# Segment-recurrent attention with streamed weights: a ring of six places and 21 units, and four output units inside the last values pass

## The chip, the cores and the metric

The kernel runs on one core of a Trainium2 chip. The metric is the device time of one execution in microseconds (us), the median of several runs. A core has a matrix engine (TensorE, PE in the profile, with its weight loads as PEld), a vector engine (DVE), a scalar engine (ACT), GpSimd (POOL) and SP, which only issues DMAs here. Results of TensorE land in PSUM banks and are moved to the on-chip memory (SBUF) by DVE or ACT; this is called evicting below.

## The reference

For x of 2048 tokens by 1024, xn is its layer norm, and the result is x + A(xn) + B(xn). B is a feed-forward block with gelu (1024 to 3584 and back). A is attention with a memory that is carried along:

```
for s in range(n_seg):                     # 64 segments of 32 tokens
    h = concat([mem, xs])                  # 8 memory rows + 32 tokens = 40 rows
    q, k, v = h Wq, h Wk, h Wv             # 32 heads of 128
    p = softmax(mask(q k^T / sqrt(128)))
    o = (p v) Wo                           # 4096 to 1024
    mem = o[:8]                            # memory of the next segment
    outs.append(o[8:])
```

The next segment needs mem, so the 64 segments run one after the other, and each reads all of Wq, Wk, Wv and Wo (32 MB in bf16).

## The kernel before

A first stage computes the layer norm and B and lays the normalised rows out for the segments (hr_d in device memory). Then come the 64 segments, which the change touches.

**Units.** The four weight matrices are cut into 64 units of 128 x 2048 (512 KB): K, Q and V have 8 units (i) in each of two halves of the heads (u), O has 16. ORDER (L46) is the order of use in a segment: K, Q, V of half 0, K, Q, V of half 1, then all of O. 44 units stay in SBUF; 20, marked S in PLACED, are streamed from device memory in every segment through a ring of STREAM_BUFS = 5 places. Ring places and resident units share the same SBUF, so one place more is one resident unit less. When a streamed unit has been used, unit_done calls start_stream (L185): SP issues the DMA of the unit five further on in the list into the place just left (L193). One streamed unit, IN_PSUM, the fourth of the list, is not fetched by DMA but copied out of PSUM by ACT (L190) and then DVE (L191).

**Rows.** Each pass works on 32 rows: the 8 memory rows and 24 of the segment's tokens. The other 8 tokens of each segment ("left" rows) don't feed the memory, and are worked on for four segments at once. With i4 the segment's number modulo 4, the left rows add a second product per unit to K (i4 = 0), to Q (2), to V (3), and make the O products twice as wide (1).

**A segment.** half_pass (L588) multiplies the rows hT by the 8 units of one matrix and half: four matmuls of 512 columns per unit side by side on TensorE (L598). `at` is a list of calls made after a given unit. Passes are evicted by rows_out (ACT, L626) or left_out (DVE, L632). turn_k and turn_q transpose (L555, L642, L652); scores multiplies q and k and takes the exponential on ACT (L696); sums adds them up, takes logarithm and exponential on ACT (L708, L709) and scales on DVE (L710, L711); values multiplies by v (L722, L728) and evicts with ACT and DVE (L734, L735). o_product (L746) adds the 16 O units up in one accumulator, psX. At the end L841 (ACT) and L842 (DVE) evict psX, L222 transposes, and L223 writes the new memory rows into hT; the next segment's K pass starts there. L847 adds the residual.

**Accumulators.** Four PSUM banks are handed out by new_acc and taken back by let_go, first in, first out. A pass whose bank has just been left waits until its eviction has ended.

**Around the change.** Each engine runs its instructions in the order in which the code writes them. Before, turn_q comes after V3 of the half 1 (the unit with i = 3), scores(1) after V6; then V is evicted on DVE, the next segment's rows are loaded on POOL's queue (load_x_rows, L201), and the O units follow, with sums after O1, values(1, 0) after O5, values(1, 1) after O7. load_res (L808) loads the residual, on POOL's queue with i4 of 0 and 3, on ACT's (after O8) with 1 and 2.

Of the kernel before, what the change touches and what calls it, by code (L numbers as in the profile page):

```python
# [17 lines left out]
S = 2048  # L18
# [23 lines left out]


NUNIT = 64
STREAMED = 20
STREAM_BUFS = 5  # L46


def pass_order():

    order = []

    for u in range(2):
        for w in ("K", "Q", "V"):
            for i in range(KT):
                order.append((w, i, u))
    for ch in range(2):
        for j in range(4):
            for u in range(2):
                order.append(("O", ch * 4 + j, u))  # L60
    return order


ORDER = pass_order()
PLACED = "S...S..." "S...S..S" "...S..S." "..S...S." ".S..S..S" "..S..S.." "S..S..S." ".S..S..S"
IS_STREAMED = {unit: PLACED[n] == "S" for n, unit in enumerate(ORDER)}
assert PLACED.count("S") == STREAMED
RESIDENT = [unit for unit in ORDER if not IS_STREAMED[unit]]
# [6 lines left out]
def kernel(  # L75
# [16 lines left out]
    nc = tc.nc  # L92
# [106 lines left out]
    def load_x_rows(s, eng=nc.sync):  # L199
        hr = hrp.tile([P, 256], BF16, name="hr")  # L200
        eng.dma_start(out=hr[:, :], in_=hr_d[s, :, 0:256])  # L201
        nxt["hT"] = hr.rearrange("p (k t) -> p k t", k=KT)
# [290 lines left out]
    with tc.tile_pool(name="late", bufs=1) as late, \  # L493
# [10 lines left out]
        def new_acc():  # L504
            bank = free_banks.popleft()
            ps = banks.tile([P, 512], F32, name="acc", tag=bank)
            bank_of[id(ps)] = bank, ps
            return ps
# [48 lines left out]
        def by_head(t):  # L557
            return t.rearrange("p c (j t) -> p (c j) t", j=4)

        O_UNITS = ORDER[48:]  # L560

        hT, hL = nxt["hT"], nxt["hL"]
        kL, VL = [None] * 2, [None] * 2
# [3 lines left out]
        for s in range(NSEG):  # L567
# [18 lines left out]
            st = {}  # L586

            def half_pass(w, u, left, at, lead=0):  # L588


                ps = new_acc()
                psL = new_acc() if left else None
                ahead = [i for i in range(KT) if not IS_STREAMED[w, i, u]][:lead] if left else []
                order = ahead + [i for i in range(KT) if i not in ahead]

                def product(i, t, lhs, acc, seq):
                    for j in range(4):
                        nc.tensor.matmul(  # L598
                            acc[32 * j:32 * j + 32, :],
                            lhsT=lhs[:, i, :],  # L600
                            rhs=t[:, 512 * j:512 * j + 512],
                            start=(i == seq[0]),
                            stop=(i == seq[-1]),
                            tile_position=(0, 32 * j),
                        )

                for i in ahead:
                    product(i, unit_tile((w, i, u)), hL, psL, order)
                for i in range(KT):
                    t = unit_tile((w, i, u))  # L610
                    product(i, t, hT, ps, range(KT))
                    if left and i not in ahead:
                        product(i, t, hL, psL, order)
                    if first and (w, i, u) == IN_PSUM:
                        keep_unit(t)
                    unit_done((w, i, u))
                    for fn in at.get(i, ()):
                        fn()
                return ps, psL
# [10 lines left out]
            def left_out(psL, tag, pool=sp):  # L630
                nat = home(tag, pool)
                nc.vector.tensor_copy(out=nat[:, :], in_=psL[:, :])  # L632
                let_go(psL)
                return nat

            def left_values(u, ps):
                VL[u] = left_out(ps, f"VL{u}", late)
# [11 lines left out]
            def turn_q(nat):  # L649
                turn4(nat, tr)  # L650
                st["qT"] = HOME["b"].rearrange("p (h q) -> p h q", q=40)
                nc.vector.tensor_copy(out=st["qT"][:, :, 0:32], in_=by_head(tr))  # L652

            def turn_qL(nat, u):
                turn4(nat, qL[:, 4 * u:4 * u + 4, :])

            def q_left(u):

                if i4 == 3 and more:
                    q = qS[:, u, :, :]  # L660
                else:
                    q = by_head(qL[:, 4 * u:4 * u + 4, :])[:, :, NL * i4:NL * i4 + NL]
                nc.vector.tensor_copy(out=st["qT"][:, :, 32:40], in_=q)

            def keep_q(u):

                nc.vector.tensor_copy(
                    out=qS[:, u, :, :], in_=by_head(qL[:, 4 * u:4 * u + 4, :])[:, :, 3 * NL:4 * NL]
                )

            def scores(u):

                kT, qT = st["kT"], st["qT"]
                sA = mixed[:, 0:160].rearrange("p (c q) -> p c q", q=40)
                sB = mixed[:, 160:224].rearrange("p (c q) -> p c q", q=16)
                for n, (o, m) in enumerate((
                    (sA[:, :, 0:NX], mask_order[:, None, 0:NX].to_broadcast([P, 4, NX])),
                    (sB, mask_seg[:, i4:i4 + 1, None].to_broadcast([P, 4, 16])),
                    (sB[:, :, 8:16], mask_order[:, None, NL * i4:NL * i4 + NL].to_broadcast([P, 4, NL])),
                )):  # L680
                    nc.tensor.matmul(o, lhsT=ident[:, :], rhs=m, start=(n == 0), stop=False, skip_group_check=True)
                for c in range(4):
                    for j in range(4):
                        q = slice(32 * j, 32 * j + 32)
                        nc.tensor.matmul(
                            sA[q, c, :], lhsT=kT[:, 4 * c + j, :], rhs=qT[:, 4 * c + j, :],
                            start=False, stop=True, skip_group_check=True, tile_position=(0, 32 * j),
                        )
                    for j in range(4):
                        q = slice(32 * j, 32 * j + 32)  # L690
                        nc.tensor.matmul(  # L691
                            sB[q, c, :], lhsT=kL[u][:, 4 * c + j, :], rhs=qT[:, 4 * c + j, NX:40],
                            start=False, stop=True, skip_group_check=True, tile_position=(0, 32 * j),
                        )
                pr = sp.tile([P, 224], BF16, name="pr", tag="e")
                nc.scalar.activation(out=pr[:, :], in_=mixed[:, 0:224], func=ACT.Exp, scale=INV_SQRT_DH)  # L696
                st["pr"] = pr
# [92 lines left out]
                at[6].append(lambda: left_values(0, psVL))  # L790
            psQ1, psQ1L = half_pass("Q", 1, left_q, at)
            natq1 = rows_out(psQ1, "b")
            at = {3: [lambda: turn_q(natq1)], 6: [lambda: scores(1)]}
            if first:
                at[3].append(lambda: st.update(natL=left_out(psQ1L, "VL1", late)))
                at[5] = [lambda: turn_qL(st["natL"], 1), lambda: q_left(1)]
            else:
                at[3].append(lambda: q_left(1))
            if left_o:
                def load_resL():  # L800
                    st["resL"] = sp.tile([P, 256], BF16, name="resL", tag="qS")
                    nc.gpsimd.dma_start(out=st["resL"][:, :], in_=hrL_d[og, :, 256:512])

                at[3].append(load_resL)

            def load_res(tag, eng):
                st["res"] = sp.tile([P, 256], BF16, name="res", tag=tag)
                eng.dma_start(out=st["res"][:, :], in_=hr_d[s + 1, :, 256:512])  # L808
# [1 line left out]


            if i4 in (0, 3) and not final and not first:
                at[4] = [lambda: load_res("qS", nc.gpsimd)]
            psV1, psV1L = half_pass("V", 1, left_v, at)
            st["V"] = left_out(psV1, "a")
            if first:
                left_values(1, psV1L)
            if not final:
                load_x_rows(s + 1, nc.gpsimd)


            at = {1: [sums], 5: [lambda: values(1, 0)], 7: [lambda: values(1, 1)]}
            if left_v and not first:
                at[7].append(lambda: left_values(1, psV1L))
            if left_q and not first:
                at[8] = [lambda: keep_q(1), lambda: st.update(natL=left_out(psQ1L, "d"))]
                at[11] = [lambda: turn_qL(st["natL"], 1)]
            psX = new_acc()
            for n, unit in enumerate(O_UNITS):
                t = unit_tile(unit)  # L830
                o_product(unit, t, psX)
                unit_done(unit)
                for fn in at.get(n, ()):
                    fn()
                if n == 8 and not st.get("res"):
                    load_res("e", nc.scalar)
            nw = 2 if left_o else 1
            if not final:
                o_sb = HOME["d"]
# [83 lines left out]
```

## Time and profile before

| what | value |
|---|---|
| median of 3 runs | 2337.02 us (2333.44 to 2340.34) |
| profiled execution, its own time | 2337.02 us |
| its span, first to last instruction | 2335.2 us |
| TensorE busy | 2072.1 us (89%) |
| DVE, ACT, POOL busy | 841.4, 656.1, 269.5 us |
| streamed and resident fetches on SP's queue | 703.15 MB of 728.35 MB |
| mean DMA rate over the span | 312 GB/s |

A group line of the profile names line, engine, operation, output and inputs, then count, busy time and mean length, then the idle time before it and what ended it. A wait line reads: who waited <- for whom: total us, times, longest. A line of the timeline is start, length, engine, line, operation, and in brackets the idle time before it and its releaser. The chain of work that ended last is followed back from the last instruction; "DMA u<-Wc_Q" is a streamed Q unit on its way into the ring (u).

### The profile page before, as it was taken

The page shows a single profiled execution, that of the slowest core. Times are in us where ns is not written, and L with a number is a line of the kernel's source. Part 1 is how long each engine was busy: PE and PEld are TensorE (multiplying, and loading weights), DVE is VectorE, ACT ScalarE, POOL GpSimd, SP SyncE. Part 2 cuts the span into 40 slices and gives each one's busy share as a digit, 9 for nine tenths or more (in the row PEclk, how much of TensorE's full clock was granted, in tenths as well). Part 3 has the DMA queues.
Part 4 walks back from the last instruction along what each step waited for, and adds up shares of the span by engine and source line. Part 5 has one row for each costly group of instructions (what it writes and reads, how often), then busy time and mean ns, then how long its engine had stood idle before and what let it go on. Part 6 is the DMA issues. An engine that isn't in the chain of part 4 may idle for free.

```text
span 2335.2 us, 78748 instructions
## 1 busy us (share of the span) xinstructions
PE 2072.1 (89%) x34687; PEld 1063.2 (46%) x34707; DVE 841.4 (36%) x2311; ACT 656.1 (28%) x1540; POOL 269.5 (12%) x527
## 2 busy tenths in 40 slices
PE   7999999888888889898889888888888888898986
PEld 3444444344444444444444444444444444444443
DVE  6574753233333333333323233333333333333332
ACT  5261532122222222222222222222222222222222
POOL 0000000033101010111010101010101111111111
PEclk9999999999999999999999999999999999999999
DMA  9521117899999999999999999999999999999997
GB/s 324 181 69 44 43 51 263 305 374 376 348 345 358 349 344 365 353 360 357 347 343 361 324 340 354 355 355 357 350 341 346 350 352 343 353 350 359 371 345 273
DMA packets 247412, 728.35 MB, mean 312 GB/s; under 512 B 49899, under 2 KB 67259, under 8 KB 247068
## 3 DMA queue, kind: packets, MB, share of 16 engines
q1 hardware_dynamic: 225532, 703.15, 82.5%
q0 software_dynamic: 16000, 16.87, 2.2%
q8 instruction: 271, 4.44, 0.7%
q10 hardware_dynamic: 5536, 3.30, 0.5%
q14 instruction: 73, 0.60, 0.1%
HBM read 708.96 MB, written 32.57 MB: 318 GB/s over the span
## 4 chain that ended last, share of the span: by engine, by line
PE 57%; DMA 33%; ACT 4%; DVE 4%; issue 2%; POOL 0%; ACTq 0%; POOLq 0%; SPq 0%; DVEq 0%
PE acc L598 26%; DMA u<-Wc_Q 13%; DMA u<-Wc_O 10%; PE ps L391 8%; PE ps L438 6%; DMA u<-Wc_K 6%; PE acc L746 6%; DMA u<-Wc_V 4%; PE mixed L555 3%; PE acc L722 2%; PE ps L471 2%; ACT u L190 1%; ACT d_oL L735 1%; ACT d_oL L734 1%; DVE u L191 1%
## 5 line engine op out<-in xcount | busy, mean ns | idle before, releaser
L598 PE MATMUL acc<-u,hr 128*32 128x512 bf16 x12288 | 968.5, 400 | 91.3 <-DMA u<-Wc_Q 36.4
L598 PEld LDWEIGHTS <-hr 128*32 128x32 bf16 x12288 | 327.5, 99 | 422.2 <-issue 179.0
L598 PE MATMUL acc<-u,hrL 128*32 128x512 bf16 x3072 | 305.6, 389 | 2.0 <-ACT xtok L484 1.1
L626 ACT CAST d_oL<-acc 128x512 bf16<-128x512 f32 x192 | 112.5, 586 | 477.6 <-PE acc L598 416.2
L391 PE MATMUL ps<-u 128*128 128x512 bf16 x896 | 196.5, 382 | 2.6 <-ACT u L297 2.6
L642 DVE COPY kT<-mixed 128x512 bf16<-128x512 bf16 x128 | 54.4, 425 | 362.8 <-PE mixed L555 361.3
L746 PEld LDWEIGHTS <-b_oL 128*32 128x32 bf16 (+1 forms) x3552 | 129.7, 113 | 83.8 <-issue 72.8
L438 PE MATMUL ps<-u 128*128 128x512 bf16 x657 | 146.2, 379 | 0.8
L746 PE MATMUL acc<-u,d_oL 128*32 128x256 bf16 (+1 forms) x2220 | 132.7, 296 | 13.4 <-DMA u<-Wc_O 11.2
L696 ACT ACTIVATE pr<-mixed 128x224 bf16<-128x224 f32 x128 | 45.8, 357 | 347.6 <-PE mixed L691 332.4
L746 PEld LDWEIGHTS <-d_oL 128*32 128x32 bf16 (+1 forms) x3552 | 125.8, 112 | 36.9 <-issue 19.0
L746 PE MATMUL acc<-W_O,b_oL 128*32 128x256 bf16 (+1 forms) x2220 | 129.9, 296 | 11.2 <-issue 11.2
L391 PEld LDWEIGHTS <-u 128*128 128x128 bf16 x896 | 88.3, 99 | 109.6 <-issue 6.2
L652 DVE COPY b_oL<-mixed 128x512 bf16<-128x512 bf16 x128 | 54.4, 425 | 210.7 <-PE mixed L555 210.7
L746 PE MATMUL acc<-u,b_oL 128*32 128x256 bf16 (+1 forms) x1332 | 90.4, 296 | 42.7 <-DMA u<-Wc_O 40.7
L555 PEld LDWEIGHTS <-d_oL 128*128 128x128 bf16 x1020 | 59.1, 98 | 123.2 <-ACT d_oL L626 47.6
L598 PEld LDWEIGHTS <-hrL 128*32 128x32 bf16 x3072 | 85.5, 98 | 62.5 <-issue 8.6
L201 POOL DMA_DIRECT2D hr<-hr_d x63 | 34.5, 548 | 666.9 <-PE acc L598 379.9
L734 ACT CAST d_oL<-acc 128x128 bf16<-128x128 f32 x128 | 51.8, 404 | 196.1 <-PE acc L728 196.1
L438 PEld LDWEIGHTS <-u 128*128 128x128 bf16 x672 | 65.3, 98 | 77.3 <-DVE g_u L407 0.4
L555 PE MATMUL mixed<-ident,d_oL 128*128 128x128 bf16 x896 | 89.2, 222 | 9.9 <-DVE d_oL L632 5.5
L191 DVE COPY u<-kept 128x1024 bf16<-128x1024 bf16 x63 | 43.6, 692 | 150.7 <-ACT u L190 145.3
(126 smaller groups left out, 2449.9 us busy)
## 6 DMA issues: line engine op xcount, KB each, us to landing
u<-Wc_O SPq DMA_DIRECT2D x384, 512.0 KB
u<-Wc_Q SPq DMA_DIRECT2D x321, 512.0 KB
u<-Wc_K SPq DMA_DIRECT2D x256, 512.0 KB
u<-Wc_V SPq DMA_DIRECT2D x256, 512.0 KB
u<-in_B_w_dram SPq DMA_DIRECT2D x16, 448.0 KB
u<-in_B_w_dram SPq DMA_DIRECT2D x14, 512.0 KB
u<-in_A_Wk_dram SPq DMA_DIRECT2D x12, 512.0 KB
u<-in_A_Wv_dram SPq DMA_DIRECT2D x12, 512.0 KB
```

The source lines that it names most:

```text
L191: nc.vector.tensor_copy(out=t[:, 1024:2048], in_=nxt["kept"][:, 1, :])
L391: nc.tensor.matmul(ps[:, :].rearrange("p (s t) -> p s t", t=SEG), lhsT=w1_sb[fb // 14 * 8 + kt][:, (fb % 14) * P:(fb % 14 + 1) * P], rhs=x ...
L438: nc.tensor.matmul(ps[:, :], lhsT=gts[fc // 4][:, fc % 4, t * P:(t + 1) * P], rhs=w2_sb[fc // 2][:, fc % 2, cs], start=(fc == 0), stop=(fc ...
L471: nc.tensor.matmul(pss[2 * t + nb][:, :], lhsT=gts[fc // 4][:, fc % 4, t * P:(t + 1) * P], rhs=w2_sb[fc // 2][:, fc % 2, nb * 512:nb * 512 ...
L555: nc.tensor.transpose(dst[:, c, :], nat[:, c * P:(c + 1) * P], ident[:, :])
L598: nc.tensor.matmul(acc[32 * j:32 * j + 32, :], lhsT=lhs[:, i, :], rhs=t[:, 512 * j:512 * j + 512], start=(i == seq[0]), stop=(i == seq[-1] ...
L626: nc.scalar.copy(out=nat[:, :], in_=ps[:, :])
L642: nc.vector.tensor_copy(out=st["kT"][:, :, :], in_=by_head(tr))
L652: nc.vector.tensor_copy(out=st["qT"][:, :, 0:32], in_=by_head(tr))
L722: nc.tensor.matmul(oV[b][:, c, :], lhsT=V[q, c * P:(c + 1) * P], rhs=prA[q, c, :], start=(c == 0), stop=False, skip_group_check=True, tile ...
L734: cp(out=(o_both if left_o else o_main)[u][:, hs, 0:32], in_=oV[b][:, :, 0:32])
L746: nc.tensor.matmul(acc[r:r + n // 8, 0:n], lhsT=lhs[:, 4 * (i % 4) + 2 * u + k, :], rhs=t[:, 1024 * k + n * jq:1024 * k + n * jq + n], sta ...
```

## The change

The ring gets six places and 21 units are streamed. The first four O units move into the V pass of half 1, one after each odd V unit; they need only heads of half 0, whose values are done by then. turn_q and scores(1) come after V2 and V4 instead of V3 and V6, sums after V6 instead of O1, values(1, 0) after O6 instead of O5. psX is taken before the V pass. V of half 1 is evicted by ACT, and ACT's queue loads the next segment's rows, ahead of that eviction. The units that are streamed are others (PLACED), and with them the one kept in PSUM: Q, 3 in place of Q, 4.

```diff
-STREAMED = 20
-STREAM_BUFS = 5
+STREAMED = 21
+STREAM_BUFS = 6
...
+    outs = [("O", ch * 4 + j, u) for ch in range(2) for j in range(4) for u in range(2)]
+    for n in range(4):
+        at = order.index(("V", 2 * n + 1, 1)) + 1
+        order[at:at] = [outs.pop(0)]
+    return order + outs
...
-PLACED = "S...S..." "S...S..S" "...S..S." "..S...S." ".S..S..S" "..S..S.." "S..S..S." ".S..S..S"
+PLACED = "S...S..S" "...S...S" "..S..S.." "S...S..S" "..S..S.S" "..S..S.." "S..S..S." ".S..S..S"
...
-            at = {3: [lambda: turn_q(natq1)], 6: [lambda: scores(1)]}
+            at = {2: [lambda: turn_q(natq1)], 4: [], 6: [sums]}
...
+            at[4].append(lambda: scores(1))
+            psX = new_acc()
...
-            psV1, psV1L = half_pass("V", 1, left_v, at)
-            st["V"] = left_out(psV1, "a")
-            if first:
-                left_values(1, psV1L)
-            if not final:
-                load_x_rows(s + 1, nc.gpsimd)
-            at = {1: [sums], 5: [lambda: values(1, 0)], 7: [lambda: values(1, 1)]}
+            at_o = {6: [lambda: values(1, 0)], 7: [lambda: values(1, 1)]}
...
+            def o_unit(n):
+                o_product(O_UNITS[n], unit_tile(O_UNITS[n]), psX)
+                unit_done(O_UNITS[n])
+                for fn in at_o.get(n, ()):
+                    fn()
+                if n == 8 and not st.get("res"):
+                    load_res("e", nc.scalar)
+
+            for n in range(4):
+                at.setdefault(2 * n + 1, []).append(lambda n=n: o_unit(n))
+            psV1, psV1L = half_pass("V", 1, left_v, at)
+            if not final:
+                load_x_rows(s + 1, nc.scalar)
+            st["V"] = rows_out(psV1, "a")
+            if first:
+                left_values(1, psV1L)
+            for n in range(4, len(O_UNITS)):
+                o_unit(n)
```

More of the change, by code (lines that the diff above doesn't have):

```diff
@@ L56, in pass_order @@
                 order.append((w, i, u))
[L57 to L61, printed above, removed]
+    outs = [("O", ch * 4 + j, u) for ch in range(2) for j in range(4) for u in range(2)]
[3 more added lines that the diff above has]
+    return order + outs
 ORDER = pass_order()
-PLACED = "S...S..." "S...S..S" "...S..S." "..S...S." ".S..S..S" "..S..S.." "S..S..S." ".S..S..S"
+PLACED = "S...S..S" "...S...S" "..S..S.." "S...S..S" "..S..S.S" "..S..S.." "S..S..S." ".S..S..S"
 IS_STREAMED = {unit: PLACED[n] == "S" for n, unit in enumerate(ORDER)}
@@ L558, in by_head @@
             return t.rearrange("p c (j t) -> p (c j) t", j=4)
-        O_UNITS = ORDER[48:]
+        O_UNITS = [unit for unit in ORDER if unit[0] == "O"]
         hT, hL = nxt["hT"], nxt["hL"]
@@ L792 @@
             natq1 = rows_out(psQ1, "b")
-            at = {3: [lambda: turn_q(natq1)], 6: [lambda: scores(1)]}
+            at = {2: [lambda: turn_q(natq1)], 4: [], 6: [sums]}
             if first:
-                at[3].append(lambda: st.update(natL=left_out(psQ1L, "VL1", late)))
-                at[5] = [lambda: turn_qL(st["natL"], 1), lambda: q_left(1)]
-            else:
-                at[3].append(lambda: q_left(1))
+                at[2].append(lambda: st.update(natL=left_out(psQ1L, "VL1", late)))
+                at[4] += [lambda: turn_qL(st["natL"], 1), lambda: q_left(1)]
+            else:
+                at[2].append(lambda: q_left(1))
+            at[4].append(lambda: scores(1))
+            psX = new_acc()
             if left_o:
@@ L802, in load_resL @@
                     nc.gpsimd.dma_start(out=st["resL"][:, :], in_=hrL_d[og, :, 256:512])
-                at[3].append(load_resL)
+                at[3] = [load_resL]
             def load_res(tag, eng):
@@ L812 @@
             if i4 in (0, 3) and not final and not first:
-                at[4] = [lambda: load_res("qS", nc.gpsimd)]
-            psV1, psV1L = half_pass("V", 1, left_v, at)
-            st["V"] = left_out(psV1, "a")
-            if first:
-                left_values(1, psV1L)
-            if not final:
-                load_x_rows(s + 1, nc.gpsimd)
-            at = {1: [sums], 5: [lambda: values(1, 0)], 7: [lambda: values(1, 1)]}
+                at[4].append(lambda: load_res("qS", nc.gpsimd))
+            at_o = {6: [lambda: values(1, 0)], 7: [lambda: values(1, 1)]}
             if left_v and not first:
-                at[7].append(lambda: left_values(1, psV1L))
+                at_o[7].append(lambda: left_values(1, psV1L))
             if left_q and not first:
[L826 to L833, printed above, removed]
+                at_o[8] = [lambda: keep_q(1), lambda: st.update(natL=left_out(psQ1L, "d"))]
+                at_o[11] = [lambda: turn_qL(st["natL"], 1)]
+            def o_unit(n):
+                o_product(O_UNITS[n], unit_tile(O_UNITS[n]), psX)
+                unit_done(O_UNITS[n])
+                for fn in at_o.get(n, ()):
                     fn()
```

## The prediction

> **What bounds the kernel now.** I read the page first (span, busy shares, the 40 slices), then TensorE's own waits, then the windows of the DMA engines, then the chain in order of time, and last the timeline around the end of one segment.
>
> ```profile
> span 2335.2 us, 78748 instructions
> PE 2072.1 (89%) x34687; PEld 1063.2 (46%) x34707; DVE 841.4 (36%) x2311; ACT 656.1 (28%) x1540; POOL 269.5 (12%) x527
> DMA  9521117899999999999999999999999999999997
> GB/s 324 181 69 44 43 51 263 305 374 376 348 345 358 349 344 365 353 360 357 347 343 361 324 340 354 355 355 357 350 341 346 350 352 343 353 350 359 371 345 273
> ...
> L190 ACT COPY u<-kept x63: 1012/1012/1014, 473.5 to 2291.9; 128x1024 bf16<-128x1024 bf16 x63
> ...
> PE acc L746 <- DMA u<-Wc_O: 51.9, 89, 2.2
> PE acc L598 <- DMA u<-Wc_Q: 36.4, 66, 1.5
> PE acc L598 <- DMA u<-Wc_K: 24.3, 34, 1.6
> PE acc L598 <- DMA u<-Wc_V: 15.4, 22, 3.3
> PE acc L746 <- issue: 13.3, 16, 2.2
> ```
>
> The copy L190 runs once per segment, so 62 periods lie between its first and last start: (2291.9 - 473.5) / 62 = 29.33 us per segment. All 64 segments come to some 1,880 of the 2,335 us, and nothing else is touched by the change. TensorE and the DMA engines both look full. TensorE's waits for streamed weights are 128.0 us plus 13.3 with no releaser shown: 2.0 to 2.2 us per segment, spread over Q, K, V and O units. Without them a segment is 29.33 - 2.1 = 27.2 us.
>
> Is the DMA side really full? Rows are window, then PE, PEld, DVE, ACT, POOL, then granted clock, DMA share, GB/s:
>
> ```profile
> 380.00:400.00 20.00, 19.89 (x92) 9.07 (x93) 0.00 (x0) 0.00 (x0) 0.00 (x0) 1.00 1.03 412
> 440.00:460.00 20.00, 14.43 (x233) 6.29 (x232) 4.72 (x11) 2.11 (x5) 0.00 (x0) 0.91 1.04 399
> 520.00:2280.00 1760.00, 1552.42 (x30698) 816.50 (x30694) 561.01 (x1603) 462.64 (x1200) 234.95 (x442) 0.96 0.96 352
> ...
> 1209.30 6.70 DMA u<-Wc_V
> 1228.96 7.15 DMA u<-Wc_K
> 1245.53 6.47 DMA u<-Wc_Q
> 1255.69 5.97 DMA u<-Wc_O
> ```
>
> It is not. When many resident units are asked for at once (380 to 400, 440 to 460) the same engines move 412 and 399 GB/s; in the segments they move 352. The last four lines, from the chain, say why: a unit is usable 6.0 to 7.2 us after its issue (mean 6.6). A place of the ring is used once per 5/20 of a segment, 7.33 us; 6.6 of it is transit, and 0.7 is left for the product, the release and the issue. The ring is the bound: SP can't ask earlier because no place is free.
>
> A rule of the Trainium skill speaks against that reading. "HBM Reference", Specifications, gives about 358 GB/s per core, and "DMA: Bandwidth & Descriptors", Where 436 GB/s comes from, lets that bind a transfer from HBM; 352 would then be the wall, and the larger stream (10.85 MB per segment, worked out below) would take 10.85 / 358 = 30.3 us per segment, 61 us more in all, 2398 us. The windows at 399 and 412 say otherwise, and the first page itself allows a core streaming alone about 425.
>
> **The change part by part.**
>
> *One unit more, one place more.* A place is then used once per 6/21 of a segment. Were the transit unchanged, the segment would be 7.33 x 21/6 = 25.7 us, so the ring stops being the only bound and the next two come up. DMA: 352 GB/s x 29.33 us = 10.32 MB per segment; 20 units fetched in place of 19 (one of the list is copied out of PSUM) add 0.52, so 10.85 MB, at 399 GB/s 27.2 us. TensorE without waits: 27.2 us. Two equal bounds that feed each other through six places don't both run full. I let half of today's wait stay, 1.0 us: the engines must then run at 10.85 / 28.2 = 385 GB/s, 96% of the sustained 399, where they run at 88% now. 28.2 against 29.33 is 1.1 us, times 62.5 segments 69 us of gain. Ends: all waits gone, 2.1 x 62.5 = 131 us gain; rate stuck at 352, 30.8 us per segment, 92 us loss. SP's one issue more per segment (0.32 us) is hidden, since SP sits waiting for places most of the time; POOL has one DMA less.
>
> *Values evicted by ScalarE behind a DMA issue.* Now the DVE cast L632 (0.69 us) starts 0.43 us after the start of pass V's last matmul (at 1227.33 in the timeline, the cast at 1227.76), and six O units and the sums lie between that and values(1, 0). After, only O3 to O6 lie there: 0.19 + 4 x 0.216 = 1.05 us (0.216 us is the spacing of two units of four matmuls). ScalarE first waits for the same matmul, issues the load of the next rows (0.33), then casts (0.59): 0.43 + 0.33 + 0.05 + 0.59 + 0.09 = 1.45 us. So TensorE waits 0.4 us where the pass has no second half, 0.2 where it has (i4 = 3), and nothing with i4 = 1, whose O units take twice as long: on average 0.25 us, 16 us in all. Below: 0, if DMA waits on O units cover it.
>
> *Sums and scores earlier.* Sums run after V6 with V7, O3 to O6 behind them, five units where there were four (O2 to O5); the row L709 ends 0.98 us and the multiplications 1.46 us after the sums start, and values now start at 1.4. Scores and turn_q keep three and four units of cover, because O1 and O0 replace V units. Cost nothing; if the cover fails, 0.1 us each. On POOL nothing waits behind the load that leaves it: what follows there are writes of results, which wait for L847.
>
> *Accumulators.* Four PSUM banks are handed out in turn. psX now takes one before psV1, so V's first product meets a bank that values(0, 1) has just left. The same meeting exists now with i4 = 3:
>
> ```profile
> 1016.72 0.30 ACT L735 CAST d_oL<-acc 128x32 bf16<-128x32 f32 x1
> ...
> 1017.07 0.40 PE L598 MATMUL acc<-u,hr 128*32 128x512 bf16 x4 [0.21 <-ACT d_oL L735]
> ```
>
> The first V product stands 0.21 us behind the cast. It comes new with i4 = 0 and 1 (0.2 us), and with i4 = 3 the second accumulator falls behind left_values, one cast of 0.70 us later (0.5 us more): (0.2 + 0.2 + 0 + 0.5) / 4 = 0.23 us, 14 us in all. Above: 0.7 everywhere, 44 us.
>
> *Switching tiles.* L598 to L746 costs nothing extra with 32 columns (0.19 us from the last V to the first O), but 0.32 with i4 = 1 and its 64 columns. Six more such changes in 16 segments at 0.11 us: 11 us. The way back, O to V, is in no row; bounds 0 and 0.11.
>
> *Next rows on ScalarE's queue.* They must be there before L223 writes into them.
>
> ```profile
> hr<-hr_d POOLq DMA_DIRECT2D x63, 64.0 KB, 5.6
> ...
> 1202.95 0.33 ACTq L808 DMA_DIRECT2D res<-hr_d  x1
> 1209.57 0.42 DVE L847 TENSOR_TENSOR res<-acc,res 128x256 bf16<-128x256 f32 x1 [1.63 <-DMA res<-hr_d]
> ```
>
> On POOL's queue they land 5.6 us after issue and L223 needs them 7.5 us after (5.8 at the least); no wait shows. After, the sums and three O units (0.38 + 0.65 us) have moved ahead of the issue, so the need comes 1.0 us sooner, 6.5 us, later by the 0.4 of the values' wait. The nearest row on ScalarE's queue is the residual of the same size: 6.6 us from issue to use in the line shown. So cover is about zero. I take 0.15 us per segment, 10 us; bounds 0 and 1.5 us per segment, 94 us. "DMA: Bandwidth & Descriptors", SWDGE vs HWDGE, calls the hardware path the faster to set up; here the residual's 6.6 stands against 5.6.
>
> *PSUM copy.* The unit kept there is now the fourth of the new list (Q, 3 instead of Q, 4); its copy is started after O9, not O12. L190 (1.01 us), then L191 (0.69), end before L842 in most segments already; L842 is some 0.1 us late in the rest. 4 us gained; ends 0 and 18.
>
> **The sum.** New work on TensorE: 16 + 14 + 11 + 10 - 4 = 47 us. While TensorE waits for something else the ring fills, so part is paid out of DMA waits that would have come anyway; both bounds being equal, I count 60%, 28 us. 2337 - 69 + 28 = 2296 us. The profiled execution took 2337.02 us, span 2335.2 and 1.8 around it, and is also the median of the three runs.
>
> **The rivals.**
> - Transfer-bound (slower): the extra unit is paid at the present rate. For: every slice reads 9 and the share is 0.96. Against: 399 and 412 GB/s. It decides if the segments can't go above 10.85 / 29.33 = 370 GB/s; at 365, 2337 + 0.4 x 62.5 = 2362 us; at 352, 2429.
> - Late rows (slower): the load on ScalarE's queue lands after the tail needs it. For: 6.6 against 6.5 us. Against: other lines of that queue may be shorter. It decides from a mean wait of 0.75 us at L223 (41 / 62.5 = 0.66, and 0.1 is counted already); at 1.2 us, 2296 + 1.1 x 62.5 = 2365.
> - Standstill: the waits of values, banks and tiles at full price (47 - 10 = 37), and half the ring's gain: 2337 - 34 + 37 = 2340. For: both bounds are as near as 27.2. Against: waits of 2.1 us leave room for both.
> - Full gain: 0.25 us of waits per segment stay (a gain of 1.85 x 62.5 = 115) and 70% of the 47 is hidden: 2337 - 115 + 14 = 2236. For: 412 GB/s is possible. Against: the stream is uneven.
>
> **How the numbers follow.** Forecast 0.50 (2255 to 2330), full gain 0.14, standstill 0.08, transfer-bound 0.16, late rows 0.12. Three runs lie within 0.15% of their median on either side, so 0.3% (7 us) is what can be told. Faster 0.64, same 0.08, slower 0.28. From 2235 to 2385 leaves out about half of the full gain and half of the transfer-bound case, under 0.2.
>
> **What would show it.** A period of L190 near 28.7 us; over 370 GB/s between 520 and the end; TensorE's DMA waits near 65 us; a wait of values (L722) on ScalarE's cast; first V products behind L735; no DMA named before L223. Wrong if the rate stays near 352 with a transit near 8 us (the ring was not the bound), or if L223 waits for hr.

## Result and profile after

The changed kernel takes 2300.71 us (median of 6 runs, 2287.09 to 2306.82) against 2337.18 us before (6 runs, 2327.14 to 2340.34): ratio 0.9843, 95% interval 0.9807 to 0.9879. The forecast was 2296 us. The profiled execution took 2305.77 us, span 2304.0.

The page of the changed kernel, the copy out of PSUM, TensorE's waits, the window of the segments, and two pieces of the chain (line numbers are one higher than before, seven higher after the V pass):

```profile
span 2304.0 us, 78841 instructions
PE 2060.4 (89%) x34687; PEld 1045.1 (45%) x34707; DVE 795.7 (35%) x2247; ACT 689.5 (30%) x1604; POOL 235.4 (10%) x464
...
GB/s 328 194 70 43 45 50 262 303 366 404 382 390 351 383 362 393 366 396 348 378 366 390 361 394 357 367 376 379 368 371 367 383 372 392 363 380 375 374 378 302
...
L191 ACT COPY u<-kept x63: 1012/1012/1013, 469.1 to 2263.6; 128x1024 bf16<-128x1024 bf16 x63
...
PE acc L747 <- issue: 25.1, 28, 2.2
...
PE acc L599 <- DMA u<-Wc_Q: 23.8, 37, 2.2
PE acc L599 <- DVE hr L224: 22.9, 47, 1.4
PE acc L599 <- DMA u<-Wc_K: 18.1, 34, 1.9
...
PE acc L747 <- DMA u<-Wc_O: 15.4, 34, 0.9
PE acc L599 <- ACT d_oL L736: 12.5, 32, 0.6
PE acc L723 <- ACT b_oL L736: 9.0, 46, 0.2
...
PE acc L599 <- DMA u<-Wc_V: 5.5, 8, 1.4
...
PE acc L723 <- ACT natL L627: 4.6, 14, 0.6
...
520.00:2280.00 1760.00, 1562.41 (x31146) 809.48 (x31138) 524.67 (x1564) 501.77 (x1279) 204.02 (x385) 0.97 0.99 376
...
1212.98 6.55 DMA u<-Wc_O
1220.02 7.67 DMA u<-Wc_K
```

The period of the copy is (2263.6 - 469.1) / 62 = 28.94 us, 0.39 us less than before. The DMA engines move 376 GB/s in the segments, where they moved 352. TensorE's named waits for weights fell from 128.0 us to 62.8 (23.8 + 18.1 + 15.4 + 5.5). In their place stand new ones: V's first products behind the casts of the values before them (L736, 12.5 us; 1.5 us before), the first K products behind the new rows (L224, 22.9; 11.3 before), values of the half 1 behind ScalarE's cast of V (L627, 4.6), the second call of values behind the casts of the first (L736 into b_oL, 9.0 us in 46 segments; no such line before), and 25.1 us at O units without a releaser (13.3 before).

The rows loaded on ScalarE's queue do come late. DVE's waits, then SP's, whose issues of streamed units (L194) are held up by the same load:

```profile
DVE hr L224 <- DMA hr<-hr_d: 19.6, 21, 1.9
...
SPq L194 <- DMA hr<-hr_d: 36.7, 31, 2.4
```

Neither line exists before the change, when L223 waited only for TensorE's transposes.

### The profile page after: what moved, and what is told of

Its sections match the earlier page's. It is cut to its first block, busy times and chain, and to the rows that moved or that the text cites. A ratio compares the mean times of both kernels' runs of the same rounds, so it can differ in the third digit from the quotient of the medians.

```text
span 2304.0 us, 78841 instructions
## 1 busy us (share of the span) xinstructions
PE 2060.4 (89%) x34687; PEld 1045.1 (45%) x34707; DVE 795.7 (35%) x2247; ACT 689.5 (30%) x1604; POOL 235.4 (10%) x464
## 4 chain that ended last, share of the span: by engine, by line
PE 65%; DMA 24%; ACT 4%; DVE 4%; issue 2%; POOL 0%; ACTq 0%; POOLq 0%; DVEq 0%; SPq 0%
PE acc L599 29%; PE acc L747 9%; PE ps L392 8%; DMA u<-Wc_Q 7%; DMA u<-Wc_O 6%; PE ps L439 6%; DMA u<-Wc_K 6%; PE mixed L556 4%; DMA hr<-hr_d 4%; PE acc L723 2%; PE ps L472 2%; ACT d_oL L735 1%; PE mixed L686 1%; ACT d_oL L736 1%; DVE d_oL L633 1%
## 5 line engine op out<-in xcount | busy, mean ns | idle before, releaser
L599 PE MATMUL acc<-u,hr 128*32 128x512 bf16 x12288 | 982.5, 393 | 88.4 <-DMA u<-Wc_Q 23.8
L599 PEld LDWEIGHTS <-hr 128*32 128x32 bf16 x12288 | 322.7, 97 | 395.4 <-issue 140.1
L627 ACT CAST d_oL<-acc 128x512 bf16<-128x512 f32 x192 | 112.3, 585 | 467.1 <-PE acc L599 396.8
L747 PE MATMUL acc<-u,d_oL 128*32 128x256 bf16 (+1 forms) x2220 | 158.9, 303 | 13.5 <-DMA u<-Wc_O 12.0
L711 DVE TENSOR_TENSOR pr<-pr,mixed 128x160 bf16<-128x160 bf16 x128 | 41.2, 322 | 257.5 <-ACT mixed L710 255.7
L892 POOL DMA_DIRECT2D out_dram<-res x124 | 63.0, 515 | 622.0 <-DVE res L854 621.9
```

The source lines that it names most:

```text
L599: nc.tensor.matmul(acc[32 * j:32 * j + 32, :], lhsT=lhs[:, i, :], rhs=t[:, 512 * j:512 * j + 512], start=(i == seq[0]), stop=(i == seq[-1] ...
L627: nc.scalar.copy(out=nat[:, :], in_=ps[:, :])
L747: nc.tensor.matmul(acc[r:r + n // 8, 0:n], lhsT=lhs[:, 4 * (i % 4) + 2 * u + k, :], rhs=t[:, 1024 * k + n * jq:1024 * k + n * jq + n], sta ...
L892: nc.gpsimd.dma_start(out=out_flat[rows, 256 * j:256 * j + 256], in_=res[32 * j:32 * j + NX, :])
```

## The experiments

**The ring alone.** The kernel before with

```diff
-STREAMED = 20
-STREAM_BUFS = 5
+STREAMED = 21
+STREAM_BUFS = 6
...
+PLACED = "S...S..S" "...S...S" "..S..S.." "S...S..S" "..S..S.S" "..S..S.." "S..S..S." ".S..S..S"
```

> Six places and 21 units streamed, at the same positions of the list as in the changed kernel, with everything else as before: O units after V, values evicted by DVE, rows on POOL's queue. My theory (the ring bounds the segment, the new order only adds waits): the ring's 69 us without the 28 us of new waits, 2337 - 69 = 2268 us, and over 376 GB/s between 520 us and the end. Rival (the gain comes from the new order, the ring and the larger stream cancel): 2337 us within 0.5%.

Measured: 2284.61 us, ratio to before 0.9779 (0.9725 to 0.9833). The busy times, the window (from 520 to 2230 us, the last value is GB/s), the copy and TensorE's waits for weights and without a releaser:

```profile
PE 2048.7 (90%) x34707; PEld 1055.8 (46%) x34707; DVE 844.2 (37%) x2311; ACT 655.3 (29%) x1540; POOL 269.6 (12%) x527
...
520.00:2230.00 1710.00, 1528.58 (x30730) 809.50 (x30723) 564.45 (x1607) 463.50 (x1205) 235.65 (x443) 0.97 1.00 381
...
L190 ACT COPY u<-kept x63: 1012/1012/1013, 473.0 to 2238.0; 128x1024 bf16<-128x1024 bf16 x63
...
PE acc L746 <- issue: 40.0, 27, 3.0
...
PE acc L598 <- DMA u<-Wc_Q: 21.2, 41, 1.6
PE acc L746 <- DMA u<-Wc_O: 19.3, 46, 1.4
PE acc L598 <- DMA u<-Wc_K: 18.8, 42, 1.3
...
PE acc L598 <- DMA u<-Wc_V: 11.9, 22, 2.7
```

The ring is the whole gain: 52 us (0.0221 x 2337), where 69 were forecast. The rate rises to 381 GB/s, the period falls to 28.47 us. The rival falls.

**The order alone.** The changed kernel with five places, 20 units and the positions of before.

```diff
-STREAMED = 21
-STREAM_BUFS = 6
+STREAMED = 20
+STREAM_BUFS = 5
...
+PLACED = "S...S..." "S...S..S" "...S..S." "..S...S." ".S..S..S" "..S..S.." "S..S..S." ".S..S..S"
```

> The changed order (four O units inside V, later calls, values on ScalarE, rows on its queue) with the ring of five places, 20 units streamed, at the positions of before. My theory: the new waits alone, 2337 + 28 = 2365 us, between 2345 and 2385. Rival (the order itself helps, since the streamed units are used more evenly and the PSUM copy leaves the tail): 2300 to 2325 us.

Measured: 2354.67 us, ratio 1.0085 (1.0058 to 1.0112).

```profile
PE acc L599 <- DVE hr L224: 15.8, 49, 1.0
...
PE acc L599 <- ACT d_oL L736: 12.9, 33, 0.6
PE mixed L223 <- DVE d_oL L849: 11.8, 37, 0.5
PE acc L723 <- ACT b_oL L736: 8.8, 45, 0.2
...
PE acc L599 <- DVE d_oL L736: 2.1, 8, 0.3
```

The order costs 20 us by itself, 28 were forecast. The two halves add up as far as the intervals tell: -52 + 20 = -32, and the change measured -0.0157 x 2337 = -37.

**Places without bytes.** Six places, still 20 units; one resident unit is left out.

```diff
-STREAM_BUFS = 5
+STREAM_BUFS = 6
...
-        late_units = deque(RESIDENT[len(RES_PLACES):])
+        late_units = deque(RESIDENT[len(RES_PLACES):-1])
...
-            return res_tiles[unit]
+            return res_tiles[RESIDENT[-2] if unit == RESIDENT[-1] else unit]
```

> The kernel before with six places and still 20 units streamed. The memory for the sixth place comes from one resident O unit, which is left out: its products read the tile of another O unit, so the same number of products and streamed bytes runs on one tile fewer. My theory (places bound it): a place is used once per 6/20 of a segment, the ring's own period falls to 7.33 x 20/6 = 24.4 us, the bound becomes TensorE's 27.2 us with some wait left, 27.8 us per segment, 2337 - 95 = 2242 us. Rival (the memory side gives no more than it gives now, 352 GB/s): no change, 2337 us within 0.5%, with a longer transit, 8.1 us in place of 6.6.

Measured: 2245.17 us, ratio 0.9605 (0.9558 to 0.9652).

```profile
520.00:2230.00 1710.00, 1541.82 (x31303) 825.07 (x31295) 576.31 (x1637) 473.03 (x1227) 235.79 (x444) 0.97 0.98 370
...
L190 ACT COPY u<-kept x63: 1012/1012/1012, 470.5 to 2198.3; 128x1024 bf16<-128x1024 bf16 x63
```

The forecast was 2242. With the same bytes per segment one more place is worth 4%, and the rate goes from 352 to 370 GB/s: the memory side was not the bound. The kernel proper pays for the sixth place with a resident unit (4 KB per partition), and so with one streamed unit more.

**Bytes without places.** Five places, 21 units, one tile unused.

```diff
-STREAMED = 20
+STREAMED = 21
...
+PLACED = "S...S..S" "...S...S" "..S..S.." "S...S..S" "..S..S.S" "..S..S.." "S..S..S." ".S..S..S"
```

> The kernel before with five places and 21 units streamed, one tile of memory unused. My theory: a place is used 21 times in place of 20 per five places, so 7.33 x 21/5 = 30.8 us per segment, 2337 + 92 = 2429 us, and the rate stays at 352 GB/s. If the waits of TensorE were rather due to where the streamed units lie, 2337 to 2360 us. Together with the run on six places it separates bytes from places: the change paid this price and bought that gain.

Measured: 2398.96 us, ratio 1.0260 (1.0200 to 1.0319), 356 GB/s.

```profile
520.00:2230.00 1710.00, 1475.65 (x28756) 762.41 (x28749) 523.72 (x1501) 432.32 (x1123) 219.17 (x413) 0.96 0.97 356
...
L190 ACT COPY u<-kept x63: 1012/1012/1012, 470.1 to 2357.2; 128x1024 bf16<-128x1024 bf16 x63
```

The forecast was 2429 us at an unchanged 352 GB/s. The time is 30 us lower and the period 30.44 us where the law of the ring (one turn of a place per 5/21 of a segment, the turn unchanged) gave 30.8. It is well above the 2337 to 2360 that the positions alone were to make. So one streamed unit more costs 61 us when places bound, and one place more is worth 92 us at 20 units (2337 to 2245) and 114 at 21 (2399 to 2285). That the change gained something is the difference of two larger numbers.

**Further along the same path.** Seven places and 22 units, evenly spread, order of before.

```diff
-STREAMED = 20
-STREAM_BUFS = 5
+STREAMED = 22
+STREAM_BUFS = 7
...
+PLACED = "S.S..S..S..S..S..S..S..S..S..S..S.S..S..S..S..S..S..S..S..S..S.."
```

> The kernel before with seven places and 22 units streamed, spread evenly, with the order of before: the next step on the same path as the change. My theory (with six places the DMA engines are near what they give, 399 GB/s, and each further streamed unit costs its bytes): 10.32 + 2 x 0.52 = 11.37 MB per segment, at 399 GB/s 28.5 us as a floor; with some wait left 28.9 us, 2337 - 27 = 2310 us, slower than six places with 21 (2285). Rival (places still bound it): 7.33 x 22/7 falls to 23 us, and it would be faster than 2285.

Measured: 2317.22 us, ratio 0.9911 (0.9880 to 0.9943).

```profile
520.00:2230.00 1710.00, 1511.24 (x30300) 797.88 (x30292) 543.73 (x1578) 446.02 (x1180) 230.46 (x433) 0.98 1.01 393
```

The forecast was 2310. At 393 GB/s the engines are within 2% of the 399 that they sustained with everything asked for at once. From six places to seven the added bytes cost more than the place brings, unlike from five to six. The positions differ too in this run, so a part may be theirs.

**Seven places, 20 units**, two resident units left out.

```diff
-STREAM_BUFS = 5
+STREAM_BUFS = 7
...
+        late_units = deque(RESIDENT[len(RES_PLACES):-2])
...
+            return res_tiles[RESIDENT[-3] if unit in RESIDENT[-2:] else unit]
```

> The kernel before with seven places and 20 units streamed; two resident O units are left out, their products read the tile of a third. With six places and the same stream the median was 2245 us, 27.87 us per segment. If TensorE's own work and the DMA rate bound it from there, a seventh place is worth little: 2225 to 2240 us. If places still bound it, transit would stay near 7.5 us, and the period would fall towards 26 us: 2130 to 2180 us.

Measured: 2221.27 us, ratio 0.9503 (0.9464 to 0.9542).

```profile
520.00:2180.00 1660.00, 1503.52 (x30784) 803.13 (x30788) 560.14 (x1609) 448.52 (x1202) 231.79 (x436) 0.98 0.99 375
...
L190 ACT COPY u<-kept x63: 1012/1012/1147, 464.1 to 2171.7; 128x1024 bf16<-128x1024 bf16 x63
...
PE acc L746 <- issue: 51.5, 32, 3.2
```

The seventh place brings 24 us where the sixth brought 92; 2225 to 2240 were forecast for the case that TensorE's own work and the rate bound it. Hardly a wait for weights is left, but the waits without releaser have grown to 51.5 us. The period, 27.54 us, is close to the 27.2 us that I had taken for TensorE without waits. Without these 51.5 us it would be 27.54 - 51.5 / 62 = 26.7 us (an estimate), so 27.2 was no floor.

**Next rows back on POOL's queue**, all else as changed.

```diff
-                load_x_rows(s + 1, nc.scalar)
+                load_x_rows(s + 1, nc.gpsimd)
```

> The changed kernel with the next rows loaded by POOL's queue again, all else as changed. In its profile DVE's L224 waits 19.6 us for the rows, and SP's issues of streamed units (L194) wait 36.7 us for their landing. My theory: both go; the first is worth 10 us or a little more, the second a part of its 36.7 us, since a streamed unit issued later comes later: 2301 - 15 = 2286 us, between 2275 and 2295. Rival (POOL's rows are as late, the need comes 1.0 us sooner whatever the queue): 2301 us within 0.3%, with L224 waiting for rows from POOL.

Measured: 2293.08 us, ratio to before 0.9816 (0.9772 to 0.9859).

```profile
DVE hr L224 <- PE mixed L223: 18.9, 55, 0.4
...
DVE hr L224 <- DMA hr<-hr_d: 6.7, 8, 1.7
```

L224's waits for rows fall from 19.6 to 6.7 us, and SP no longer waits for them at all. The median is 8 us lower; the intervals of this run and the changed kernel overlap, so no gain in time is shown. SP's part of the mechanism is: its waits are 27.1 to 36.7 us in the three profiles with six places and the rows on ScalarE's queue (the changed kernel and the next two runs), and nothing in the two with the rows on POOL's (this run and both repairs together). L224's part is weaker, since with the rows still on ScalarE's queue its wait is 8.3 and 12.2 us in the next two runs and 5.3 in the order alone. In the packed trace the rows land a median 5.9 us after issue in the changed kernel and 5.4 here. The rival had a point too: 6.7 us of waiting stay on POOL's queue; that this is because the need comes sooner was not tried by itself.

**Accumulator taken after the V pass's.**

```diff
-            psX = new_acc()
...
             def o_unit(n):
+                if n == 0:
+                    st["psX"] = new_acc()
```

> The changed kernel with psX taken from the four banks after the V pass has taken its own, just before the first O unit, so that V gets the bank it got before. My theory: the waits of V's first products for L736 and L633 (12.5 + 1.5 + 1.4 us, 1.5 before) go; 60% of the 14 us is paid out: 2301 - 8 = 2293 us. Rival (the wait for the bank moves to psX, which then gets the bank just left): no change, and the first O product waits for L736 instead.

Measured: 2285.97 us, ratio 0.9790 (0.9748 to 0.9831). V's waits for L736 fall from 12.5 to 0.6 us, and the first O product waits 0.8 + 1.0 us instead, so the rival's wait exists and is small. The median is 15 us lower, as much as the wait itself and more than the 60% that I had allowed. But the intervals of this run and the changed kernel overlap here too: that the wait goes is shown, the size in time is not. L224's wait for the rows is also smaller here, with the rows on the same queue.

```profile
PE acc L747 <- ACT b_oL L627: 1.0, 2, 0.6
...
PE acc L747 <- ACT d_oL L736: 0.8, 3, 0.3
...
PE acc L599 <- ACT d_oL L736: 0.6, 3, 0.2
...
DVE hr L224 <- DMA hr<-hr_d: 8.3, 11, 1.3
```

**Values evicted by DVE again.**

```diff
-            st["V"] = rows_out(psV1, "a")
+            st["V"] = left_out(psV1, "a")
```

> The changed kernel with the V pass of half 1 evicted by DVE again; rows still on ScalarE's queue. My theory: values no longer wait for L627 (4.6 us in 14 segments): -3 us, 2298 us, within 0.3% of the changed kernel. Rival (the eviction on DVE falls behind the scaling of the sums, L711 and L712, and comes later than on ScalarE): 2301 to 2315 us, with values waiting for DVE.

Measured: 2294.44 us, ratio 0.9833 (0.9793 to 0.9872): no difference to the changed kernel that can be told. The rival's wait is there all the same.

```profile
PE acc L723 <- DVE natL L633: 12.0, 28, 0.6
```

Values wait 12.0 us for DVE where they waited 4.6 for ScalarE. With the sums moved ahead, DVE is scaling them when V ends: in all 64 segments its cast of V starts directly behind L712. By this wait ScalarE is the better place; the times don't show it.

**Both repairs together** (rows on POOL's queue, accumulator after V).

> The changed kernel with psX taken after the V pass's banks and the next rows loaded by POOL's queue. The two runs that did one each gained 15 and 8 us against the changed kernel's 2301. If they cost different places of the segment, they add up: 2278 us, between 2270 and 2286, a little under the ring alone (2285). Rival (TensorE's waits only change their name, since the DMA side now sets the pace): 2286 us, no better than the one of the two alone, with the waits for u units grown by what the others lost.

Measured: 2283.91 us, ratio 0.9772 (0.9738 to 0.9806), the lowest of the versions that leave nothing out, and not to be told from the ring alone (2284.61) or the accumulator alone (2285.97). Whether the repairs add up stays open. The waits for weights and those without releaser:

```profile
PE acc L747 <- issue: 26.9, 26, 2.5
PE acc L747 <- DMA u<-Wc_O: 26.5, 57, 1.2
...
PE acc L599 <- DMA u<-Wc_K: 22.5, 50, 1.1
PE acc L599 <- DMA u<-Wc_Q: 20.8, 34, 1.6
```

Their named part, the waits for weights, is 73.4 us with V's 3.6, against 62.8 in the changed kernel: part of what the repairs took away came back as waits for weights, as the rival had it. With both repairs the new order is worth no more than leaving it out.

**Half the instructions at O.** The waits without releaser are explained below; these two runs were made for them. In the ring alone, and in the kernel before, each O unit where i4 is not 1 takes four matmuls of 512 columns.

```diff
-                (w, i, u), n = unit, 512 if left_o else 256
+                (w, i, u), n = unit, 512
...
-                        r = n // 8 * jq
+                        r = 64 * jq if left_o else 64 * k + 32 * jq
+                        m = 64 if left_o else 32
...
-                            acc[r:r + n // 8, 0:n],
+                            acc[r:r + m, 0:n],
```

> The ring alone (2284.61 us), with each O unit where i4 is not 1 multiplied by four matmuls of 512 columns in place of eight of 256: the same products and the same time on TensorE (0.216 us), half the instructions. The two partial sums, k = 0 and k = 1, then stand in different rows of psX, and adding them is left out. In the ring alone TensorE waits 40.0 us at O units without a releaser, and goes on each time 1.2 to 1.6 us after a read of 16 KB on the instruction queue. If it runs out of instructions there: the waits fall under 10 us, the reads from 271 to about 248, and 25 us of the 40 are paid out, 2260 us, between 2245 and 2270. Rival (these are waits for weights whose releaser the profile lost): they stay near 40 us and the time near 2285.

> The same edit in the kernel before (five places, 20 units), where these waits are 13.3 us and places bound the pace; the sum of the two halves is left out again. If instructions are what is late, the 13.3 us go and little is gained, since the next unit is then waited for instead: 2329 us, between 2320 and 2337. If the shorter instruction stream helped in some other way (less to issue, fewer weight loads), the gain would be as large here as with the ring of six, 25 us: 2312.

Measured: 2236.67 us with the ring (ratio to before 0.9580, 0.9547 to 0.9614), 2325.33 us without (0.9953, 0.9930 to 0.9977). Of the kernel with the ring, the window, the queue of instructions and the longest waits:

```profile
520.00:2180.00 1660.00, 1500.12 (x27751) 725.84 (x27747) 561.85 (x1601) 462.02 (x1200) 232.35 (x437) 0.99 1.01 392
...
q8 instruction: 248, 4.06, 0.7%
...
PE acc L747 <- DMA u<-Wc_O: 38.1, 74, 1.2
...
PE acc L598 <- DMA u<-Wc_K: 23.2, 50, 1.1
```

And of the one without it, the longest wait:

```profile
PE acc L747 <- DMA u<-Wc_O: 78.5, 105, 2.3
```

In both kernels no wait of over 0.5 us without releaser is left. The rival of the first falls. With the ring the gain is 48 us, more than the 40 us of these waits, and their end is not all of it. TensorE's waits for weights rise from 71.2 to 92.7 us, and its busy time falls from 2048.7 to 2019.6 us, most of that at the O products, whose groups add up to 443 us in the ring alone and 415 here. The matmuls of 256 columns on W_O took 293 ns on average in the ring alone and 279 in the kernel before, so late instructions may lengthen them too; that is not shown. A part may be the clock, 0.985 granted over the run against 0.974 in the ring alone. Without the ring the gain is 12 us. That it is close to the 13.3 that went is chance: the waits for weights rise by 22 us (128.0 to 150.0), as was expected where places bound the pace, and the busy time falls by 16 (2072.1 to 2056.1). So the waits without releaser are accounted for, and the times only in part. This form would need the two halves added before it computes the reference; that was not tried.

## Why the prediction was right

- **The bound.** Shown: places, not bytes, bound the kernel before (2245 us with a place and no bytes, 2399 with bytes and no place). The slower rival, a wall at the rate of before, falls with 376 to 393 GB/s in the segments. With it falls the reading of "HBM Reference", Specifications, that a core is held to about 358 GB/s, as far as a core alone is meant; that page's own remark on a core streaming alone is the one that agrees. One reading of the prediction was too high: the four transits of 6.6 us on average come from the chain, which picks late units. Over all streamed units after 560 us, the packed trace gives 6.1 us from the issue to the last of a unit's 16 completion counts, five sixths of the 7.33 us and not nine tenths.
- **The ring's term** was too large: 69 forecast, 52 measured alone, and a part of the 52 is luck. TensorE's named waits for weights did fall to about half, from 128.0 us to 62.8 in the changed kernel and 71.2 in the ring alone. But the 13.3 us without releaser, which I had added to them, are waits for instructions; they grew to 25.1 us, and to 40.0 with the ring alone, so that 27 us of the ring's gain were given back there. Of the 141.3 us that I halved, 111.2 are left in the ring alone, a gain of 30. The other 23 us are TensorE's busy time, 2072.1 to 2048.7 us, which the sum held fixed at 27.2 us per segment; the run with a place and no bytes has 2029.0. The rate, 376 GB/s, stayed below the 385 of the sum.
- **The sum**, 2296 us against 2301, is closer than its terms. The ring's gain was 17 us too large and the cost of the order 8 us too large, and these two errors partly cancel.
- **The granted clock** stands in no term, and it is a rival that the experiments don't separate. It was 0.976 to 0.985 in the six runs of the changed kernel, and 0.959 to 0.974 in all 52 runs of the kernel before that were made beside the experiments (2323.7 to 2351.2 us). Among these 52 the time falls by 1.6 us per 0.001 of clock. If that held above 0.974 too (an estimate), 21 of the 37 us would go with the clock and 17 would be left at an equal clock; of the ring alone (0.975 on average) 13 of 52, of the place without bytes (0.976) 15 of 92. The higher clock goes with the places: no run of a kernel with five places had more than 0.974, none with six or seven had less. Whether it rises because TensorE stops less, or for another reason, no run shows. The spread of the 52, 1.2%, also says that 0.3% was too little for what can be told.
- **The period** was to be near 28.7 us and was 28.94. The transit of all units, as above, grew from 6.1 to 6.6 us, and a place is now used every 28.94 x 6/21 = 8.3 us, so 1.7 us are left for product, release and issue where 1.2 were.
- **Accumulators:** 14 us forecast; 12.5 and 1.5 us in the waits for L736 on ScalarE and DVE, against 1.5 before. The mechanism was right and the wait was near its size; its price in time is not shown (15 us by medians, in overlapping intervals).
- **Values behind ScalarE:** 16 us forecast, 4.6 measured, the term that was most over-sized. I had put the DMA issue ahead of the cast as serial time. ScalarE's timeline in one segment shows it run beside the exponential:

```profile
1682.08 0.29 ACT L710 ACTIVATE mixed<-mixed 128x160 f32<-128x160 f32 x1
1682.16 0.36 ACTq L202 DMA_DIRECT2D hr<-hr_d  x1
1682.56 0.58 ACT L627 CAST natL<-acc 128x512 bf16<-128x512 f32 x1 [0.20 <-issue]
```

  The issue costs the cast 0.20 us of idle time, not 0.33 and a hand-over. In the same segment the O unit ahead of values waits 0.81 us for its weights, which covers the rest.
- **The second call of values** was given no cost, and has one: 9.0 us in the changed kernel, 8.8 in the order alone. values(1, 0) moved from O5 to O6 and values(1, 1) stayed behind O7, so one O unit lies between them in place of two, and the second needs a bank before the casts of the first have ended (read from the code and the waits; not tried by itself).
- **Next rows:** 10 us forecast; L224 waits 19.6 us in 21 of 63 segments, TensorE's wait for L224 rises by 11.6, and the run without it is 8 us lower, with overlapping intervals. A wait for hr there was one of the prediction's own signs of being wrong, and it came; the 0.75 us per segment of the late-rows rival is far off (19.6 / 63 = 0.31). TensorE's part had the right size, but half of the mechanism was missing: SP's issues wait for the same landing, 36.7 us in all. I had looked at what is queued behind the load on ScalarE and POOL, and took SP to be untouched by a DMA that it does not issue.
- **PSUM copy:** 4 us forecast; the waits of L222 for DVE's L842 were 6.7 us and are 2.8. The size was right. It belongs to the ring's half of the change, with its other kept unit: the ring alone has 2.8 us, the order alone 11.8.
- **Switching tiles** (11 us) was not tried by itself; it is somewhere in the 20 us of the order alone.
- **The 60%** fits the order alone: its new waits are 4.5 us for the rows, 13.5 for banks, 10.4 for values and 5.1 for the PSUM copy, 33.5 in all; the waits for weights fall by 17.5 (128.0 to 110.5), and 20 us are paid. The terms were others than forecast, and TensorE's busy time also rose by 8 us (2080.3), so one run is no proof of the share.

## What to carry to other kernels

A busy share of 0.96 on the DMA engines was no saturation: compare the rate with a stretch of the same trace in which more is asked for at once, and compare the transit of one load with the time for which its place is held. Where a place is in transit for most of its turn (here 6.1 of 7.3 us), one place more can pay for the extra bytes until the rate meets that other stretch; here from five to six, not to seven in the one placement tried. A DMA moved to another queue can hold back a third engine that never issued it, so look for its landing in every queue's waits. And a wait that the profile gives no releaser is not to be added to the nearest class of waits: here it was instructions, not weights. Last, compare TensorE's busy time and granted clock too, and not its waits alone: they moved with the kernel here.

## What the runs showed of the hardware that was not expected

**TensorE runs out of instructions.** The waits without a releaser at the O units were 13.3 us before, 25.1 in the changed kernel, 40.0 with the ring alone, 51.5 with seven places and 20 units. The packed trace has 271 reads of 16 KB on the queue that the page calls "q8 instruction", some four per segment. In every wait of TensorE without releaser of over 0.5 us after 560 us (11 before, 22 in the changed kernel, 25 with the ring alone, 28 with seven places and 20 units) it goes on 1.2 to 1.6 us after one of these reads has landed; such stretches after a read are only some 5% of the time. The reads fit TensorE's instructions: 69,394 matmuls and weight loads before, 256 per read. The O units are where its instructions are densest: 16 in 0.216 us (eight weight loads and eight matmuls), against eight for a K, Q or V unit. With eight instead of 16 the reads fall to 248 and the waits are gone. The two findings together show the cause. They grow as the weights wait less, and with four O units spread over the V pass there are fewer of them: 20.9 to 27.4 us in the five kernels with six places and the new order, 40.0 and 41.5 in the two with the order of before. "Runtime: NRT & Kernel Launch", Instruction fetch mechanics, has instructions refilled in blocks of 16 KiB, as these runs show, and calls the cost of crossing from one to the next mostly hidden. Here it was not: up to 3.2 us at a time.

**A load on one queue holds up another.** A 64 KB load that ScalarE issues made SP, which has a queue of its own, wait for its landing 31 times, up to 2.4 us each; issued by POOL, the same load did not, and neither did ScalarE's in the order alone, with its five places. The waiting instruction names two DMA semaphores, and one of them is that of the load. In the trace the loads of SP and ScalarE take turns on the same eight semaphores, and POOL's use eight others. That fits a wait of SP for a semaphore that it is to use again; it would then come from how the compiled program hands out semaphores, not from the queues. No run tried this.
